# Loading the attention inputs two tokens to a row instead of four, so that VectorE's transposes write every second element

## The chip, the cores and the metric

The kernel runs on one core of a Trainium2 chip. The metric is the device time of one execution in microseconds, lower is better. Times of the kernel before are the median of three runs; the traces are single executions taken by the hardware profiler.

## The reference

A gated linear attention (a state of 48 x 48 for each head, decayed by `f` and fed with `k v`) is followed by a SwiGLU feed-forward block. There are 4 batch elements, 8 heads, 768 tokens of 48 channels; the feed-forward block has 3072 tokens, a width of 384 and a hidden width of 1536. All data are float32.

```python
f = 1.0 / (1.0 + np.exp(-f_logit))
for t in range(S):
    state = f[:, :, t, :, None] * state + np.einsum('bhd,bhe->bhde', k[:, :, t], v[:, :, t])
    y[:, :, t] = np.einsum('bhd,bhde->bhe', q[:, :, t], state)
x = y.transpose(0, 2, 1, 3).reshape(B * S, H * D)
g = x @ w_gate
out = (g * (1.0 / (1.0 + np.exp(-g))) * (x @ w_val)) @ w_out
```

## The kernel before

**Tiling.** The 768 tokens are cut into six chunks of 128, numbered 0 to 5. A unit is one chunk of one batch element; this document writes unit (2,0) for chunk 2, batch element 0. The attention of a unit works on channels by tokens: each of the tensors f, k and q lies as 128 partitions (two heads of 48 channels, padded to 64) by four head pairs by 128 tokens. Decays within a chunk are cumulative products (the scans at L577 and L601), scores are kT by qT products on TensorE (tile `sc`, L620), masked by VectorE (L633), and the result goes into `xT`, the transposed input of the feed-forward block. The state is carried from chunk to chunk (tile `decayed`, L541; update L708).

**Bringing tokens to channels.** In memory a token's 48 channels are contiguous. For chunks 0 and 1, f, k and q are loaded token by token (L433) and transposed by TensorE (L552). From chunk 2 on (`c >= SQUARES`) they are loaded into three rooms named `squares`, one for each of f, k and q and shared by all units, so that VectorE can transpose them in squares of 32 x 32 (L566 for f, L573 for k, L604 for q). A room row holds, for each head pair, a run of four successive tokens (`NI = 4`, 192 numbers); partition t of 32 holds tokens 4t to 4t+3. Four DMAs fill a room, one for each of four groups of 32 partitions (two heads, two halves of the channels), each with 32 partitions by 4 head pairs. VectorE's transpose turns the t of a square into the free dimension, so a square's 32 outputs are tokens i, 4+i, 8+i and so on: it writes every fourth element of a row (`in_turn`). The sigmoid of f is taken by ACT on the loaded room (L557), before the transpose.

**Loads.** `load_after(u)` follows the transpose of q of unit u in program order. It asks SP for f, then k, then q of unit u + 1. Each goes into the room that unit u's transpose of the same tensor has just read, and SP waits for that. All loads of this kind, the DMAs that copy a unit's result `yT` to `xT` (L669, ten for each of batch elements 0 to 2), the loads of v (L433), half of the output (L1067), and for six units the way of kT through DRAM (`turn`, L597, and back as `kt`, L629), are issued by SP in one fixed order. Each DMA also takes the next of eight completion semaphores in turn, over SP's and ACT's DMAs together, and waits until the DMA that had it before has landed.

For batch element 3 the result comes by another way: `decayed` is spread into a tile `diagonal` (cleared by POOL at L545, filled by ACT at L547), which feeds the y matmuls of L679. `diagonal` and `yT` are tiles of the same name in a pool of one buffer, so the clearing waits until the DMAs of L669 have read batch element 2's `yT`.

For turned units, kT is transposed by VectorE into qT's buffer (L594), sent to DRAM from there, and q's transpose (L604) may overwrite that buffer only after the four DMAs of L597 have landed.

**The feed-forward block.** For chunks 1 to 5, each of four groups of hidden columns is computed with fifteen smaller products (L959) on sums of tokens and of weights; ACT copies the results out of PSUM (L964), VectorE adds them up (L860, L863), ACT applies the SiLU (L975) and VectorE multiplies (L911). The down projection has seven products (L1058, L1121), whose results ACT and VectorE also add up. The sums of tokens of a chunk (`xs`, L860 to L866) are made by VectorE just before the chunk's first product.

**The order.** While TensorE computes the feed-forward block of chunk c - 1, the attention of chunk c is woven in by hand: `CHAINS`, `SCORES` and `times` give each step of a unit a place in TensorE's time line. From chunk 1's feed-forward on, `in_order` fixes the order of the instructions of PE, DVE, ACT, POOL and SP as written.

Of the kernel before, what the change touches and what calls it, by code (L numbers as in the profile page):

```python
# [289 lines left out]
def short_path(ctx, tc, ident, least, judge, q, k, v, f_logit, moe_w_gate, moe_w_val, moe_w_out, out):  # L290
# [9 lines left out]
    nc = tc.nc  # L300
    B, H, S, D = q.shape
    C = 128
    NCH = S // C
    HP = H // 2
# [90 lines left out]
    Q = 32  # L395
    NI = C // Q
    RUN = NI * D

    rooms = {}
# [6 lines left out]
    def v_of(u):  # L406
        return vs[u % (NV if units[u][1] < SQUARES else NV // 2)]

    def squares(nm):
        return rooms[nm][:, Q:Q + HP * RUN].rearrange("t (a i e) -> t a i e", a=HP, i=NI)[:, :, :, 0:Q]  # L410

    def in_turn(t):

        return t.rearrange("p a (t i) -> p a i t", i=NI)

    def load(u, what="fkqv"):
        b, c = units[u]
        rows = slice(c * C, (c + 1) * C)
        for nm, src in (("f", f_logit), ("k", k), ("q", q), ("v", v)):
            if nm not in what:  # L420
                continue
            if nm == "v":
                dst = v_of(u)
            elif c < SQUARES:
                dst = raw[nm][u % NRAW]
            else:
                for n in range(4):
                    at = Q * (1 - n % 2)
                    nc.sync.dma_start(
                        out=rooms[nm][Q * n:Q * (n + 1), at:at + HP * RUN].rearrange("t (a e) -> t a e", a=HP),  # L430
                        in_=src[b, n // 2::2, rows, :].rearrange("a (t i) d -> t a (i d)", i=NI))
                continue
            nc.sync.dma_start(out=dst[:, :, 0:D], in_=src[b, :, rows, :].rearrange("h t d -> t h d"))  # L433

# [95 lines left out]
    def attention(u):  # L530
# [25 lines left out]
        if c >= SQUARES:  # L556
            nc.scalar.activation(squares("f"), squares("f"), AF.Sigmoid)  # L557
            if b == (c > SQUARES):

                nc.scalar.activation(spare, spare, AF.Silu)  # L560
        else:
            p = transposed("fTp", fr)
            nc.scalar.activation(pairs(gate)[:, :, 1:N1], p, AF.Copy if u in ahead else AF.Sigmoid)
        yield
        if c >= SQUARES:
            nc.vector.transpose(in_turn(pairs(gate)[:, :, 1:N1]), squares("f"))  # L566
# [5 lines left out]
        if c >= SQUARES:  # L572
            nc.vector.transpose(in_turn(kT), squares("k"))  # L573
# [29 lines left out]
        if c >= SQUARES:  # L603
            nc.vector.transpose(in_turn(qT), squares("q"))  # L604
            load_after(u)
# [96 lines left out]
        if c >= SQUARES and u + 2 < len(units):  # L702
            load(u + 2, "v")
# [7 lines left out]
    def load_after(u):  # L711

        w = u + (1 if units[u][1] >= SQUARES else 2)
        if w < len(units) and (units[w][1] >= SQUARES) == (w == u + 1):
            load(w, "fkqv" if units[w][1] < SQUARES or w == SQUARES * B else "fkq")
# [449 lines left out]
    for u in range(NRAW):  # L1165
        load(u, "fkq")
# [198 lines left out]
```

## Time and profile before

| | us |
|---|---|
| median of three runs | 612.46 (612.24 to 613.02) |
| profiled execution, first to last instruction (its span) | 611.2 |
| TensorE busy in the span | 594.2 |
| VectorE busy | 499.2 |
| ACT busy | 286.7 |
| issue of one load of L429 on SP, median | 0.43 |
| landing of a load of L429 after its issue, median of f, k, q | 2.7, 2.6, 2.3 |

Of the profiled execution the trace gives the span and no time around it; the median of the timed runs is 1.26 us above the span, and this difference is used below where a span is turned into a time. Times in the trace are counted from the first instruction. Chunk 0 fills the first 147 us together with the loading of the weights; the feed-forward blocks of chunks 1 to 5 follow, about 93 us each. In a chunk the fifteen-product part comes first, then the down part. The loads that the change touches run from 137 to 471 us.

A row of the timeline gives start, duration, engine, line, operation, tiles, and in brackets how long the engine had been idle and what ended that. A row of the groups gives the count, then after the bar the summed time in us, the mean of one in ns, and the idle time before them. "x4" on SP merges four issues.

### The profile page before, as it was taken

The numbers are of one execution on the slowest core, as the hardware profiler recorded it, in microseconds if no ns is written. First come the engines' busy times: TensorE is split into PE (matmuls) and PEld (weight loads), VectorE is DVE, ScalarE is ACT, GpSimd is POOL, SyncE is SP. The second block draws the span as 40 slices with busy tenths as digits, with TensorE's granted clock in tenths as the row PEclk, the third lists the DMA queues.
The fourth block names the chain that finished last, engine by engine and source line by source line (L and its number), as shares of the span: only waits on it lengthen the run. The fifth ranks groups of instructions, "written<-read, shape, count | busy, mean of one in ns | idle before, by whom it ended". The sixth has DMA issues, their size and how long they took to land.

```text
span 611.2 us, 10816 instructions
## 1 busy us (share of the span) xinstructions
PE 594.2 (97%) x4036; PEld 487.9 (80%) x4036; DVE 499.2 (82%) x882; ACT 286.7 (47%) x530; POOL 7.6 (1%) x52
## 2 busy tenths in 40 slices
PE   7799999999999999999999999999999999999996
PEld 4654545566888799888899988899988899988896
DVE  7999989878999996999996889996879991566731
ACT  2465646313776522476732366742276730366600
POOL 1000000000000000000000000000000000000000
PEclk9999999999999999999999999999999999999999
DMA  9999582005323134424235344145313100100001
GB/s 149 249 213 284 174 250 79 1 14 154 89 52 69 27 95 113 118 54 96 53 95 122 104 111 111 31 114 118 105 51 90 27 6 10 53 1 2 0 1 58
DMA packets 109143, 54.10 MB, mean 89 GB/s; under 512 B 68761, under 2 KB 102169, under 8 KB 109081
## 3 DMA queue, kind: packets, MB, share of 16 engines
q1 hardware_dynamic: 107064, 50.56, 34.6%
q10 hardware_dynamic: 2016, 2.75, 1.2%
q8 instruction: 34, 0.56, 0.4%
q14 instruction: 29, 0.23, 0.1%
HBM read 44.04 MB, written 6.29 MB: 82 GB/s over the span
## 4 chain that ended last, share of the span: by engine, by line
PE 67%; DVE 9%; DMA 3%; issue 3%; ACT 3%; SPq 2%; ACTq 0%; POOL 0%; DVEq 0%; POOLq 0%
PE o L1058 15%; PE A L959 14%; PE B L959 11%; PE o L959 5%; PE o L780 5%; PE c L959 5%; PE o L1121 3%; PE sc L620 3%; PE y L658 2%; SPq L669 1%; DVE c L863 1%; PE y L679 1%; PE y L654 1%; PE dS L699 1%; DMA xT<-yT 1%
## 5 line engine op out<-in xcount | busy, mean ns | idle before, releaser
L1058 PE MATMUL o<-w_out,h 128*128 128x192 f32 x360 | 62.0, 327 | 0.5 <-DVE h L911 0.5
L959 PE MATMUL A<-xs,w_both 128*128 128x256 f32 x240 | 62.1, 381 | 0.0
L1058 PEld LDWEIGHTS o<-w_out,h 128*128 128x128 f32 x360 | 58.7, 190 | 1.7 <-DVE h L911 0.8
L964 ACT COPY c<-A 128x512 f32<-128x512 f32 x40 | 23.4, 584 | 61.3 <-PE A L959 61.3
L959 PEld LDWEIGHTS A<-xs,w_both 128*128 128x128 f32 x240 | 44.9, 190 | 6.5
L860 DVE TENSOR_TENSOR c<-c,aside 128x512 f32<-128x512 f32 x60 | 41.7, 694 | 9.8 <-ACT aside L964 8.4
L964 ACT COPY aside<-A 128x512 f32<-128x512 f32 x60 | 35.1, 586 | 30.9 <-PE A L959 30.9
L911 DVE TENSOR_TENSOR h<-h,c 128x256 f32<-128x256 f32 x100 | 41.3, 422 | 6.9 <-ACT h L975 6.8
L975 ACT ACTIVATE h<-c 128x256 f32<-128x256 f32 x100 | 39.4, 418 | 9.5 <-DVE c L860 5.8
L863 DVE TENSOR_TENSOR c<-c,aside 128x512 f32<-128x512 f32 x60 | 41.5, 692 | 2.0 <-ACT aside L964 1.7
L959 PE MATMUL B<-xs,w_both 128*128 128x256 f32 x160 | 41.2, 380 | 0.8 <-ACT aside L964 0.8
L1058 PE MATMUL o<-ws,h 128*128 128x192 f32 x240 | 41.5, 328 | 0.2 <-DVE A L633 0.2
L959 PE MATMUL c<-xT,w_both 128*128 128x256 f32 x160 | 41.2, 380 | 0.5 <-DVE c L863 0.5
L959 PE MATMUL A<-xs,extra 128*128 128x256 f32 x160 | 41.2, 380 | 0.0
L959 PE MATMUL B<-xT,extra 128*128 128x256 f32 x160 | 41.1, 379 | 0.0
L964 ACT COPY aside<-B 128x512 f32<-128x512 f32 x60 | 35.1, 586 | 11.4 <-PE B L959 6.9
L1058 PEld LDWEIGHTS o<-ws,h 128*128 128x128 f32 x240 | 39.1, 190 | 0.8 <-DVE A L633 0.4
L633 DVE TENSOR_TENSOR A<-sc,causal 128x512 f32<-128x512 f32 x48 | 30.8, 684 | 9.9 <-PE sc L620 9.8
L863 DVE TENSOR_TENSOR c<-o,c 128x512 f32<-128x512 f32 x40 | 27.8, 694 | 10.3 <-ACT h L975 5.8
L959 PEld LDWEIGHTS B<-xs,w_both 128*128 128x128 f32 x160 | 30.2, 190 | 5.2 <-ACT aside L964 1.2
L959 PEld LDWEIGHTS c<-xT,w_both 128*128 128x128 f32 x160 | 30.3, 190 | 5.0 <-DVE c L863 0.9
L959 PEld LDWEIGHTS A<-xs,extra 128*128 128x128 f32 x160 | 30.3, 190 | 4.4 <-ACT c L964 0.3
(140 smaller groups left out, 1138.8 us busy)
## 6 DMA issues: line engine op xcount, KB each, us to landing
fsquares<-in_f_logit_dram SPq DMA_DIRECT2D x64, 96.0 KB, 2.7
ksquares<-in_k_dram SPq DMA_DIRECT2D x64, 96.0 KB, 2.6
qsquares<-in_q_dram SPq DMA_DIRECT2D x64, 96.0 KB, 2.3
v<-in_v_dram SPq DMA_DIRECT2D x24, 192.0 KB, 3.2
w<-in_moe_w_gate_dram SPq DMA_DIRECT2D x6, 768.0 KB, 6.4
w<-in_moe_w_val_dram SPq DMA_DIRECT2D x6, 768.0 KB, 5.3
w<-in_moe_w_out_dram SPq DMA_DIRECT2D x6, 768.0 KB, 5.7
out_dram<-ob ACTq DMA_DIRECT2D x14, 192.0 KB, 2.3
```

The source lines that it names most:

```text
L620: nc.tensor.matmul(sc[par][:, a * C:(a + 1) * C], lhsT=kT[r, a, :], rhs=qT[r, a, :], start=True, stop=True)
L633: nc.vector.tensor_tensor(A[:, par], sc[par].rearrange("p (a t) -> p a t", t=C), causal.unsqueeze(1).broadcast_to((128, HP, C)), ALU.mult)
L658: nc.tensor.matmul(place(a, par), lhsT=v_[:, 2 * a + par, :], rhs=A[:, par, a, :], start=False, stop=a >= HP - 2, skip_group_check=True)
L780: nc.tensor.matmul(p, lhsT=hidden_tile(h, n // 2)[:, n % 2 * 2 + b // 2, b % 2 * C:(b % 2 + 1) * C], rhs=w_out[:, j, :], start=(n == 0), s ...
L860: nc.vector.tensor_tensor(dst, a, b, ALU.add)
L863: nc.vector.tensor_tensor(dst, a, b, ALU.subtract)
L911: lagging.append(lambda: f(*args))
L959: nc.tensor.matmul(p[name][:, n, :], lhsT=weights_of[a][:, n, j, :], rhs=tokens[b], start=fresh and n == 0, stop=True, skip_group_check=True)
L964: nc.scalar.copy(t, p[name])
L975: nc.scalar.activation(dst, src[:, 0, :], AF.Silu)
L1058: nc.tensor.matmul(p[:, n, :], lhsT=lhsTs[j][:, n * C:(n + 1) * C], rhs=rhs[:, j, :], start=first and j == order[0] and n == 0, stop=j == ...
L1121: nc.tensor.matmul(p, lhsT=hidden_tile(h, j)[:, 2, n * C:(n + 1) * C], rhs=b22[:, j, :], start=j == order[0], stop=j == order[-1])
```

## The change

A half chunk of 64 tokens is loaded at a time. Partition t of 32 then holds tokens 2t and 2t+1 of the first half and the same of the second, next to each other, so that a row in the room is as long as before. A contiguous run in memory is two tokens, 384 bytes, where it was four, 768. Each of f, k and q of a unit is loaded by eight DMAs instead of four, each with half the bytes and the same number of rows. A square's 32 outputs are tokens i, 2+i, 4+i and so on of one half: the transposes write every second element. Squares, transposes and everything after them have the same sizes and the same order. The loads for 16 units (chunks 2 to 5) are 384 DMAs where they were 192.

```diff
     def squares(nm):
-        return rooms[nm][:, Q:Q + HP * RUN].rearrange("t (a i e) -> t a i e", a=HP, i=NI)[:, :, :, 0:Q]
+        return rooms[nm][:, Q:Q + HP * RUN].rearrange("t (a j i e) -> t a j i e", a=HP, j=2, i=NI // 2)[:, :, :, :, 0:Q]
 
     def in_turn(t):
 
-        return t.rearrange("p a (t i) -> p a i t", i=NI)
+        return t.rearrange("p a (j t i) -> p a j i t", j=2, i=NI // 2)
...
                 for n in range(4):
                     at = Q * (1 - n % 2)
-                    nc.sync.dma_start(
-                        out=rooms[nm][Q * n:Q * (n + 1), at:at + HP * RUN].rearrange("t (a e) -> t a e", a=HP),
-                        in_=src[b, n // 2::2, rows, :].rearrange("a (t i) d -> t a (i d)", i=NI))
+                    to = rooms[nm][Q * n:Q * (n + 1), at:at + HP * RUN].rearrange("t (a j e) -> t a j e", a=HP, j=2)
+                    for j in range(2):
+                        some = slice(c * C + j * C // 2, c * C + (j + 1) * C // 2)
+                        nc.sync.dma_start(out=to[:, :, j, :],
+                                          in_=src[b, n // 2::2, some, :].rearrange("a (t i) d -> t a (i d)", t=Q))
```

## The prediction

> **What bounds the kernel now.** I read the page's busy shares first, then the busy time by stretches, then the chain of waits, and only then single engines.
>
> ```profile
> PE 594.2 (97%) x4036; PEld 487.9 (80%) x4036; DVE 499.2 (82%) x882; ACT 286.7 (47%) x530; POOL 7.6 (1%) x52
> ```
>
> TensorE is busy 97% of 611.2 us. All that a faster VectorE can bring is TensorE's idle time, so the question is where that lies. The answer by stretches (us; busy time of PE, weight loads, DVE, ACT, POOL; clock; DMA share; GB/s):
>
> ```profile
> 137.00:215.00 78.00, 76.14 (x457) 62.02 (x453) 73.85 (x128) 46.60 (x89) 0.56 (x6) 1.00 0.30 77
> 215.00:246.00 31.00, 30.73 (x295) 29.01 (x292) 23.94 (x41) 6.56 (x14) 0.63 (x3) 1.00 0.48 114
> 246.00:307.00 61.00, 61.00 (x394) 52.29 (x393) 57.05 (x106) 39.19 (x76) 0.21 (x2) 1.00 0.32 77
> ```
>
> The changed loads run from 137 to 471 us. From 246 us TensorE has no gap. Only in 137 to 215 does it lose 1.86 us, and there VectorE is busy 73.85 of 78. TensorE's own rows name what ended those gaps:
>
> ```profile
> 194.43 1.13 PE L959 MATMUL B<-xs,w_both 128*128 128x256 f32 x4 [0.75 <-ACT aside L964]
> 201.21 1.13 PE L959 MATMUL c<-xT,w_both 128*128 128x256 f32 x4 [0.47 <-DVE c L863]
> 210.76 1.57 PE L1058 MATMUL o<-w_out,h 128*128 128x192 f32 x8 [0.50 <-DVE h L911]
> ```
>
> The ACT copy in the first row itself waited 2.16 us for a VectorE sum, so all three are VectorE backlog. Next the chain of waits (start, us, what), around the last batch element of chunk 2:
>
> ```profile
> 228.21 0.65 ACT fsquares L557
> 228.85 0.32 SPq L669
> ...
> 234.45 0.59 SPq L669
> 235.04 0.04 issue
> 235.08 1.80 DMA xT<-yT
> ...
> 237.06 0.43 POOL diagonal L545
> ...
> 237.52 0.36 ACT diagonal L547
> ...
> 237.92 2.12 PE y L679 x56
> ```
>
> The tile `diagonal` shares one buffer with `yT`. POOL may clear it only when ten DMAs have copied `yT` away, and TensorE's y matmul waits for it. TensorE's previous row is 2.11 us from 235.73, so it ends at 237.84: nothing is to spare. What SP did before those ten:
>
> ```profile
> 222.82 1.95 SPq L429 DMA_DIRECT2D fsquares<-in_f_logit_dram  x4
> 224.87 1.80 SPq L429 DMA_DIRECT2D ksquares<-in_k_dram  x4
> 226.77 1.80 SPq L429 DMA_DIRECT2D qsquares<-in_q_dram  x4
> 228.66 7.01 SPq L669 DMA_DIRECT2D xT<-yT  x10
> ```
>
> `yT` was ready at 225.93 (ACT's copy, 0.77 from 225.16). The ten DMAs began 2.7 us later because SP was issuing the twelve loads of unit (3,0). The changed build keeps that order: f, k and q of (3,0), now 24, stand ahead of the ten.
>
> [...] Groups by shape (busy, mean ns of one):
>
> ```profile
> L604 DVE STREAM_TRANSPOSE qT<-qsquares 128x512 f32<-128x512 f32 x16 | 18.1, 1129 | 6.1 <-DMA turn<-qT 6.1
> L594 DVE STREAM_TRANSPOSE qT<-kT 128x512 f32<-128x512 f32 x6 | 4.2, 705 | 0.0
> L474 DVE SCALAR_TENSOR_TENSOR top<-w,top 128x768 int32<-128x768 int32 x6 | 5.7, 954 | 0.1
> L860 DVE TENSOR_TENSOR hs<-h 128x768 f32<-128x768 f32 x10 | 9.6, 962 | 0.0
> ```
>
> [...] writes 16 bytes apart take 1129 ns, contiguous ones 705. L474 reads every second word and is no slower than L860, which reads none so; a write of every second word is not in the trace. [...] an issue on L429 takes 0.43 us (median), its data land 2.3 to 2.7 us later. [...] a run of four tokens is 768 B, one of two 384 B. DMA share is at most 0.48 in the stretches above and the bytes stay the same, so I charge nothing for it, and up to 1 us for the range.
>
> **The change, part by part**, against the profiled execution (span 611.2; the median is 612.46, and I add the 1.26 at the end).
>
> *Transposes.* 48 (16 units, f, k, q) go from 1.12 us (mean of 1115, 1117 and 1129) to some 0.71, as L594: 48 x 0.41 = 19.7 us of VectorE. Bounds: nothing gained, or all. Where VectorE isn't the limit this is worth nothing, which from 246 us on is everywhere. In 146 to 211 the chain runs through VectorE; nine transposes lie there, 3.7 us, but TensorE can return no more than it loses: the three gaps above, 1.7, and 0.54 at 160.09 (matmul sc waits for qT). With what is lost in matmuls stretched to 1.13 I take at most 2.6 (four triples of fifteen products at 0.86 are 51.6, attention matmuls 5.5, the recurring short stall 0.14 x 4; 57.7 of 59.8 from 147.7 to 207.5, and 0.5 at 210.76).
>
> *The first k load.* Every DMA takes one of eight completion semaphores in turn, ACT's too, and waits for the DMA eight before it. In the new build k's fifth and seventh DMA of unit (2,0) get those of ACT's first and second output (L802). SP's f load at 148.50 stood on the first of them, so k's fifth goes at 148.5, its seventh near 149.6, its last near 150.4, landing (2.3) near 152.6. k's transpose started at 151.16, so VectorE is held 1.4 us; three shorter transposes give back 0.8 before sc at 160.09 (f's is lost in an ACT wait at 150.56). Sc is thus late by about 0.6, and TensorE with it. Of the 2.6 the 0.54 is then not regained, so about 1.9 is, and the stage nets 0.6 - 1.9 = -1.3. Bounds: -2.6 (k lands in time), +0.5 (it lands 2 us later).
>
> *Twelve more issues before xT at 228.66.* A half load has as many rows (32 partitions x 4) as a whole one. Issue time does not follow bytes: L669 moves 8 to 24 KB and takes 0.59, v 192 KB and 0.53. So each half costs SP what a load does: 1.95 + 1.80 + 1.80 = 5.55 more, and the ten start at 234.2. All behind shifts: last landing, POOL, ACT, y at 243.4. The third of the ten took 1.38 against 0.59, perhaps waiting behind the loads; that 0.8 may vanish. I take **+5.3**; bounds 4.5 and 5.6. Behind y on TensorE are dS, the last down products and the next chunk's first product, so the shift runs to the end.
>
> *The same place at chunks 3 and 4.* There xT was not held by loads: at 315.32 and 408.78 it started when `yT` was done. Chunk 3: f and k of (4,0) from 305.56 take 3.9 each, q then 3.6, so xT starts near 316.9. It took 7.26 for ten, of which 0.7 to 1.3 is a wait that is then over, so kt and turn come 0.4 late. Turn holds the q transpose, which ended in sc at 333.08 with nothing to spare; the shorter transpose repays 0.4. Behind it f and k of (4,1) issue until 336.7, and k's transpose is held from 335.74 to 338.9, with the token sums behind it on VectorE: 339.89 becomes about 341.9, first needed at 342.07. In all **+0.3**; bounds 0 and 2. Chunk 4: xT 1.5 late, POOL clears at 418.1 where y comes at 424.09; k's transpose 1.6 late, the sums on time. Nothing.
>
> *Elsewhere* f, k and q wait for data that were long there (q of (4,1) waits for turn), and ACT's later sigmoids lie in idle time (7.25 us of waiting at 332.80). The added semaphore waits, two more instructions a transpose at 0.05 us, pass while VectorE works off earlier operations; uncovered, 48 x 0.1 = 4.8 us of VectorE, again in its slack.
>
> *Sum:* -1.3 + 5.3 + 0.3 = +4.3. Span 615.5; time 612.46 + 4.3 = **616.8 us**.
>
> **The rivals.**
> 1. *Transposes gain, the queue does not bite* (0.10). If a half load's issue took under 0.11 us, twelve would cost less than the 1.3 gained. For it: VectorE bounds 146 to 211. Against: 0.43 for every L429 issue, whatever the tensor, and 0.5 to 0.6 for lines of fewer bytes. Time, at no cost of the queue and a gain of 1.3 to 2.6: 612.46 - 2.0 = 610.5. It decides if y at 237.92 comes no later than now.
> 2. *Every second element is as slow as every fourth* (0.10). No write in the trace excludes it. Then VectorE's 1.4 us of waiting for k stays: +1.4 + 5.3 + 0.3 = 619.5.
> 3. *SP falls behind at every chunk* (0.15): k and f of the next unit land 2 us later than I work out, and token sums are late at 342 and 435. +0.5 + 5.5 + 2.5 + 2 = 623. For it: f and k issues of 4.11 and 4.91 us at 326.62 and 418.36, and SP's rows from 342 to 435 add up to 60 of 93 us, with 48 more issues at 0.45 to 82. Against: that still fits, and worked through by SP's rows no load there lands more than 0.3 us after it is wanted.
> 4. *Gain and cost cancel* (0.04): 612.5, if k is in time and part of the ten DMAs' wait vanishes.
>
> **How the numbers follow.** The forecast has 0.61. Its own bounds give -2.6 + 4.5 = +1.9 to +0.5 + 5.6 + 2 + 1 = +9.1, the inner part of it 614 to 619. With rival 2 inside and rivals 1 and 3 mostly outside the range is 613.5 to 620.5. Under 0.2% (1.2 us) a measurement of this kernel can't be told from no change. Faster 0.10, same 0.04, slower 0.86.
>
> **What would show it.** Transposes near 0.71 us; 24 issues of about 0.43 to 0.49 ahead of xT; y of the last unit of chunk 2 some 4 us later, with TensorE idle about 5 before it and released by ACT's diagonal copy; k's first transpose waiting for its DMA; no new gap from 250 us but under 1 near 340. I am wrong if TensorE has no gap before that y, if a half load's issue is near 0.2, or if new gaps stand in 342 to 524.

## The result, and the profile after

| | before | after |
|---|---|---|
| median of five runs, us | 612.53 (612.24 to 613.02) | 628.87 (627.55 to 631.89) |
| ratio, 95% interval | | 1.0268 (1.0249 to 1.0287) |
| span of the profiled execution, us | 611.2 | 625.8 |
| VectorE busy, us | 499.2 | 482.8 |

The changed kernel is slower by 16.4 us (2.68% of 612.5), where 4.3 was predicted. VectorE's busy time has indeed fallen, by chance also by 16.4 us (the durations of the 48 transposes add up to 33.9 us where they were 53.8), and TensorE idles more. The busy shares of the changed kernel:

```profile
PE 597.4 (95%) x4036; PEld 489.2 (78%) x4036; DVE 482.8 (77%) x882; ACT 286.1 (46%) x530; POOL 7.5 (1%) x52
```

The load is now L432, and all lines behind it are two higher than before (the transposes are L568, L575, L606). Its transposes by shape (busy, mean ns of one, idle time ahead of them and what ended it):

```profile
L575 DVE STREAM_TRANSPOSE kT<-ksquares 128x512 f32<-128x512 f32 x16 | 11.3, 708 | 4.8 <-DMA qsquares<-in_q_dram 2.9 <-DMA ksquares<-in_k_dram 2.0
L606 DVE STREAM_TRANSPOSE qT<-qsquares 128x512 f32<-128x512 f32 x16 | 11.2, 700 | 12.7 <-DMA fsquares<-in_f_logit_dram 9.1 <-issue 3.6
```

Every second element is written as fast as a contiguous row (700 ns, where the contiguous writes of L596 take 703 here; every fourth element took 1129 before for the same tensor). But the idle time ahead of them has grown: q's transposes waited 6.1 us for `turn` before and now wait 12.7.

Where TensorE idles, by stretches (busy time of PE, weight loads, DVE, ACT, POOL; clock; DMA share; GB/s):

```profile
137.00:215.00 78.00, 73.92 (x406) 59.66 (x406) 68.96 (x126) 43.94 (x85) 0.40 (x5) 1.00 0.33 77
215.00:246.00 31.00, 25.15 (x238) 23.68 (x236) 20.25 (x35) 5.87 (x12) 0.57 (x3) 0.98 0.31 68
342.00:401.00 59.00, 55.88 (x382) 48.06 (x376) 46.05 (x90) 31.93 (x60) 0.32 (x3) 1.00 0.42 98
```

TensorE loses 4.1, 5.9 and 3.1 us in these. Before, it lost 1.9 in the first and next to nothing from 246 us on. In the first stretch VectorE is busy for 4.9 us less than before, and yet TensorE has lost time. What TensorE waited for (us in total, times, longest):

```profile
PE y L681 <- ACT diagonal L549: 5.7, 1, 5.7
...
PE kt L626 <- DVE state L710: 1.7, 1, 1.7
...
PE A L961 <- ACT c L966: 1.3, 1, 1.3
PE o L1060 <- ACT ob L1086: 1.2, 2, 0.7
PE o L1123 <- DVE c L862: 1.2, 1, 1.2
```

Only the first of these was predicted. SP's rows ahead of it look as the prediction drew them:

```profile
224.71 3.85 SPq L432 DMA_DIRECT2D fsquares<-in_f_logit_dram  x8
228.65 4.19 SPq L432 DMA_DIRECT2D ksquares<-in_k_dram  x8
232.94 3.70 SPq L432 DMA_DIRECT2D qsquares<-in_q_dram  x8
236.74 6.21 SPq L671 DMA_DIRECT2D xT<-yT  x10
```

24 issues of some 0.49 us each stand ahead of the ten `xT` DMAs, which start 8.1 us later than before.

The delay can be followed through the run. The table gives the start of the same TensorE rows after, minus their start before (us, from the time lines of the two profiled executions):

| row | first product of chunk 1 | sc (2,0) | sc (2,2) | y (2,3) | sc (3,0) | sc (4,0) | sc (4,1) | sc (4,2) | sc (5,0) |
|---|---|---|---|---|---|---|---|---|---|
| after | -0.63 | +0.76 | +1.83 | +7.41 | +8.55 | +9.64 | +12.26 | +13.96 | +14.75 |

These are single executions, the fastest of five for the changed kernel. The delay grows in four places: in chunk 1's products (2.5 us up to sc (2,2)), at y (2,3) (5.6), just behind it (1.1), and from the end of chunk 3's units through those of chunk 4 (6.2 between sc (3,0) and sc (5,0)).

Two of the waits come from no queue. On ACT the sigmoid of unit (2,0), with the table load behind it, stood ahead of chunk 0's output copies before:

```profile
141.56 0.63 ACT L557 ACTIVATE fsquares<-fsquares 128x512 f32<-128x512 f32 x1 [4.25 <-DMA fsquares<-in_f_logit_dram]
...
148.97 0.59 ACT L964 COPY c<-A 128x512 f32<-128x512 f32 x1 [0.89 <-PE A L959]
```

Now it stands behind them. ACT's rows after:

```profile
148.49 0.63 ACT L559 ACTIVATE fsquares<-fsquares 128x512 f32<-128x512 f32 x1 [1.05 <-DVE ob L803]
149.14 1.28 ACT L562 ACT_TABLE_LOAD   x1
...
150.54 0.57 ACT L966 COPY c<-A 128x512 f32<-128x512 f32 x1
```

The first product of chunk 1 is done before 148.5, but the copy that has to read its PSUM bank (a piece of the memory that TensorE writes its results to) before the fourth product adds to it comes at 150.54, and TensorE idles 1.33 us for it. Chunk 0's output copies are not in the hand-fixed order, which begins with this sigmoid, and the scheduler placed the two differently against each other. And `kt` of unit (2,1) was given the PSUM bank of `dS` of unit (2,0), which VectorE's state sum L710 frees late. Before, it had another of the three banks of its pool. Nothing in the diff names either, and the sentence above that everything after the transposes keeps its order doesn't hold for ACT.

### The profile page after: what moved, and what is told of

Read it like the earlier page. It is cut to its first block, busy times and chain, and to the rows that moved or that the text cites. A ratio compares the mean times of both kernels' runs of the same rounds, so it can differ in the third digit from the quotient of the medians.

```text
span 625.8 us, 11120 instructions
## 1 busy us (share of the span) xinstructions
PE 597.4 (95%) x4036; PEld 489.2 (78%) x4036; DVE 482.8 (77%) x882; ACT 286.1 (46%) x530; POOL 7.5 (1%) x52
## 2 busy tenths in 40 slices
DMA packets 136793, 54.13 MB, mean 86 GB/s; under 512 B 120984, under 2 KB 129816, under 8 KB 136728
## 4 chain that ended last, share of the span: by engine, by line
PE 64%; DVE 9%; SPq 7%; ACT 3%; issue 3%; DMA 1%; ACTq 0%; DVEq 0%; POOL 0%; POOLq 0%
PE A L961 15%; PE o L1060 12%; PE B L961 12%; PE c L961 5%; PE o L961 5%; PE o L782 5%; SPq L432 4%; PE o L1123 3%; PE sc L622 3%; SPq L671 2%; PE y L660 2%; DVE c L865 1%; PE y L681 1%; PE y L656 1%; PE dS L701 1%
## 5 line engine op out<-in xcount | busy, mean ns | idle before, releaser
L862 DVE TENSOR_TENSOR c<-c,aside 128x512 f32<-128x512 f32 x60 | 41.0, 683 | 10.0 <-ACT aside L966 8.5
L865 DVE TENSOR_TENSOR c<-c,aside 128x512 f32<-128x512 f32 x60 | 40.9, 682 | 2.1 <-ACT aside L966 1.8
L961 PEld LDWEIGHTS B<-xT,extra 128*128 128x128 f32 x160 | 30.2, 190 | 5.5 <-ACT c L966 1.3
```

The source lines that it names most:

```text
L862: nc.vector.tensor_tensor(dst, a, b, ALU.add)
L865: nc.vector.tensor_tensor(dst, a, b, ALU.subtract)
L961: nc.tensor.matmul(p[name][:, n, :], lhsT=weights_of[a][:, n, j, :], rhs=tokens[b], start=fresh and n == 0, stop=True, skip_group_check=True)
```

## The experiments

Each kernel ran beside the kernel before on the same chip; a ratio is to that, with its 95% interval. 0.001 is 0.6 us; differences in us between runs are worked out from the ratios.

### Half loads in one chunk at a time

The layout is chosen for each unit by a condition, so that part of the units are loaded and transposed as before. The diff is that of chunk 2; the others have `c == 3`, `c == 4` and `c == 2 and b > 0`:

```diff
+    def halved(u):
+        b, c = units[u]
+        return c == 2
...
+                    if not halved(u):
+                        nc.sync.dma_start(
+                            out=rooms[nm][Q * n:Q * (n + 1), at:at + HP * RUN].rearrange("t (a e) -> t a e", a=HP),
+                            in_=src[b, n // 2::2, rows, :].rearrange("a (t i) d -> t a (i d)", i=NI))
+                        continue
```

> Half loads and two-token rows for units (2,1), (2,2) and (2,3) alone; every other unit is loaded and transposed as before. ACT's order stays that of the kernel before (the sigmoid of unit (2,0) ahead of chunk 0's output copies), while the score transposes kt of unit (2,1) take the PSUM bank they take in the changed kernel. Theory (the cost of the changed kernel is a sum of local ones): nothing is lost at the start of chunk 1's products and nothing at the diagonal; the gain of shorter transposes in 146 to 211 us is largely eaten by the wait of kt of unit (2,1) for a bank (1.7 us). Time 611.5 to 613. As my prediction had this stage: about 1.9 us faster, 610.3 to 611.2. If each doubled load costs wherever it is: slower, above 613.5.

> Half loads for all four units of chunk 2, none later. The same as the run for (2,1) to (2,3), but unit (2,0) is also loaded in halves, and with that ACT's order becomes that of the changed kernel: the sigmoid of (2,0) stands behind chunk 0's output copies. Theory: the late sigmoid costs 1.5 to 2.5 us at the start of chunk 1's products, so 613.5 to 615.5, and some 2 us above the run without (2,0). Rival (my prediction's reason: only the ring of completion semaphores delays k): at most 0.5 us above the run without (2,0).

> Half loads for the four units of chunk 3 alone. Twelve more issues stand ahead of xT of unit (2,2), and nine groups of twelve more in chunk 2's products. Theory: 5.6 us of waiting for the diagonal, 1.1 us of slower y matmuls after that idle time, 0.3 elsewhere: +7, 619.5, bounds 618.5 to 620.5. Rival (the y matmuls were slow by chance): 618. Rival (SP's backlog from chunk 2's own half loads is part of the wait): below 617.

> Half loads for the four units of chunk 4 alone. Theory: SP falls behind where chunk 3 is handed to chunk 4 and through chunk 3's products: 0.8 before the first scores of chunk 4, 2.6 before its second y, 1.7 by the end of the products: +5, 617.5, bounds 615.5 to 618.5; q's transposes of (4,0), (4,1) and (4,2) wait for turn and f's for loads. My prediction had 0.3, so 612.8. Rival (the loss there is carried over from backlog of chunks 2 and 3): below 614.

| half loads in | ratio | us |
|---|---|---|
| (2,1), (2,2), (2,3) | 1.0020 (1.0011 to 1.0029) | +1.2 |
| chunk 2 | 1.0046 (1.0033 to 1.0060) | +2.8 |
| chunk 3 | 1.0136 (1.0120 to 1.0153) | +8.3 |
| chunk 4 | 1.0087 (1.0072 to 1.0102) | +5.3 |

Chunks 2, 3 and 4 add up to 16.4 us, all of the 16.4 of the change, to within some 2 us by the intervals. The losses are local: chunk 4 alone costs its 5.3 without any backlog from chunks 2 and 3. That refutes the rivals of the last two runs. Chunk 5's loads had no run of their own. They are not quite free: in the changed kernel TensorE falls back by 0.8 us between sc (4,2) and sc (5,0), 0.53 of it in one wait, where the run with chunk 4 alone loses nothing. In the profile of the chunk 3 run the gap before y (2,3) is 6.04 us and sc (3,0) comes 7.04 late; its measured +8.3 is a little above the theory's bounds.

The chunk 2 runs went worse than the theory: three units with faster transposes and nothing behind them to delay, and still slower than before. TensorE's rows in the run with (2,1) to (2,3):

```profile
182.21 0.88 PE L638 MATMUL kt<-idf,kT 128*128 128x128 f32 x4 [1.73 <-DVE state L722]
182.88 1.92 PE L973 MATMUL A<-xs,w_both 128*128 128x256 f32 x4
184.59 1.66 PE L973 MATMUL B<-xs,w_both 128*128 128x256 f32 x4
```

The wait of `kt` for its bank is there, and the two products behind it take 1.92 and 1.66 us where they take 1.03. These slow products are no part of the median: the profiled execution was the slowest of 13, 2.8 us above their median, and in the run with all of chunk 2 the same wait is followed by products of 1.03 us. That each doubled load costs something wherever it is would also give +1.2; the next section tells the two apart. Adding unit (2,0) costs 1.6 us more (1.0046 against 1.0020, with some 1.0 of uncertainty), as the theory of the late sigmoid had it: in that run ACT has the order of the changed kernel, and the interval between the first product of chunk 1 and sc (2,0) is 1.4 us longer than before.

### The bank and ACT's order, put back

The bank of each tile of the three-bank pool can be set by hand: three tags of one buffer each, and a list of what the other build had chosen.

```diff
+    BANKS = "576576576576756765765675675675675675675675675675675"
+    taken = []
     def bank(name):
...
+        taken.append(name)
+        return banks[-1].tile([128, 512], FP32, tag="b" + BANKS[len(taken) - 1], name=name)
```

For ACT, the order of the sigmoid, the table load, chunk 0's output copies and DMAs and the first copy of chunk 1's products is fixed as it was:

```diff
                 nc.scalar.activation(spare, spare, AF.Silu)
+                if u == SQUARES * B:
+                    keep_order([traced[-1], *out_steps])
```

> The run with half loads for (2,1) to (2,3), with one thing undone: each tile of the pool of three PSUM banks gets, by name, the bank it has in the kernel before, so that kt of unit (2,1) no longer takes the bank of dS of (2,0). Theory (the bank is what eats the gain): kt waits for nothing, its 1.73 us go, and the slow products after it (1.92 and 1.66 us for 1.03) go too; what is left is the gain of the shorter transposes, 0.8 to 1.9 us under the kernel before: ratio 0.997 to 0.9987. Rival (the shorter transposes gain nothing even so, since VectorE's backlog comes from other work): ratio 0.9995 to 1.0005. Rival (the three units' own 36 more issues cost): ratio stays at 1.002.

> The kernel before with nothing changed but the bank of each tile of that pool: those of the changed kernel. Theory: kt of unit (2,1) waits some 1.9 us for VectorE's state sum of (2,0); VectorE catches up meanwhile, so that TensorE's later gaps of 0.75, 0.47 and 0.50 shrink, and the end is 0.5 to 1.9 later: ratio 1.001 to 1.003. Rival (the wait only takes the place of the later gaps): ratio 1.000.

> The changed kernel with all its half loads, with the two side effects of scheduling undone: the sigmoid of (2,0) stands ahead of chunk 0's output copies on ACT again, and the banks are those of the kernel before. Theory: the start of chunk 1's products loses nothing (1.4 us less), kt of (2,1) waits for nothing (1.8 us less), and all else stays: some 3 us under the changed kernel, ratio to the kernel before 1.020 to 1.0235, and the first L1060 down product of chunk 1 starts 0.5 to 2 us earlier than in the kernel before. Rival (k of (2,0) is late whatever ACT does): 1.5 to 2 us under it, and the score matmul of (2,0) still waits 0.6 or more.

| | ratio |
|---|---|
| (2,1) to (2,3) halved, old banks | 0.9989 (0.9980 to 0.9998) |
| kernel before, new banks | 1.0034 (1.0021 to 1.0047) |
| changed kernel, old banks and old ACT order | 1.0199 (1.0172 to 1.0226) |

The banks alone, with no load and no transpose changed, cost the kernel before 2.1 us, more than expected. TensorE's rows of that run:

```profile
180.96 0.63 PE L630 MATMUL kt<-idf,kT 128*128 128x128 f32 x4 [1.73 <-DVE state L714]
...
196.25 1.13 PE L965 MATMUL B<-xs,w_both 128*128 128x256 f32 x4 [0.72 <-ACT aside L970]
...
203.02 1.13 PE L965 MATMUL c<-xT,w_both 128*128 128x256 f32 x4 [0.45 <-DVE c L869]
...
212.57 1.57 PE L1064 MATMUL o<-w_out,h 128*128 128x192 f32 x8 [0.51 <-DVE h L917]
```

The last three are the gaps of 0.75, 0.47 and 0.50 us that the prediction called VectorE backlog. VectorE has been given 1.7 us to catch up here, and they are still 0.72, 0.45 and 0.51. They are not a backlog that is carried along, then, but short chains between neighbouring steps (a sum, a copy, a product) that follow TensorE wherever it is.

With the old banks the three faster units gain 0.7 us instead of losing 1.2. So 36 more issues alone cost nothing here; that the transposes gain is only just clear of the noise in this run. The changed kernel with both effects undone stands 0.7% (4.2 us by the ratios, with 2.0 of uncertainty; 3.2 by its sc (5,0), which starts 12.24 late from a first product 0.09 late) below the changed kernel. There sc (2,2) is 0.8 us earlier than before. The rival of a late k of (2,0) falls: its scores come 0.2 us nearer to the first product than before.

### The number of DMAs against the size of their runs

```diff
-                    nc.sync.dma_start(
-                        out=rooms[nm][Q * n:Q * (n + 1), at:at + HP * RUN].rearrange("t (a e) -> t a e", a=HP),
-                        in_=src[b, n // 2::2, rows, :].rearrange("a (t i) d -> t a (i d)", i=NI))
+                    to = rooms[nm][Q * n:Q * (n + 1), at:at + HP * RUN].rearrange("t (a e) -> t a e", a=HP)
+                    for j in range(2):
+                        nc.sync.dma_start(
+                            out=to[:, 2 * j:2 * j + 2, :],
+                            in_=src[b, n // 2 + 4 * j:n // 2 + 4 * j + 3:2, rows, :].rearrange("a (t i) d -> t a (i d)", i=NI))
```

> The kernel before with each of the 192 loads split in two by head pairs: the layout, the runs of four tokens (768 bytes), the transposes of every fourth element, ACT's order and the PSUM banks stay those of the kernel before; only the number of DMAs doubles, as in the change. Theory (the number of issues, not the size of a run, is what costs): the diagonal, chunk 3 and chunk 4 cost what they cost in the changed kernel, and nothing is repaid by shorter transposes: ratio 1.019 to 1.026. Rival (runs of 384 bytes, twice as many packets, are to blame): 1.005 to 1.012.

Measured: 1.0241 (1.0225 to 1.0256), nearly the 1.0268 of the whole change, with runs of 768 bytes and the slow transposes. The gap before y (2,3) is 5.71 us, sc (5,0) 13.00 late. The number of issues is what costs, not the shorter runs: the DMA packets are 112217 here, 109143 before and 136793 in the changed kernel. This build also kept ACT's order and the banks of the kernel before: what moved those was the new layout, not the doubling. Against the changed kernel with those two undone (1.0199), which differs from it in the layout, the new layout, with its shorter transposes, is worth 2.6 us over the whole run, with some 1.9 of uncertainty.

### SP's order at the diagonal

```diff
-            load_after(u)
+            if (b, c) == (B - 1, 2):
+                load(u + 1, "f")
+            else:
+                load_after(u)
...
                     f += n
+            if (b, c) == (B - 2, 2):
+                load(u + 2, "kq")
```

This is the second of the three; the third has "fk" and "q" in these places, and the first put off the call of unit (2,2) as a whole.

> The changed kernel with one move on SP: the 24 loads of unit (3,0) are issued behind the ten xT DMAs of unit (2,2), not ahead of them. Theory: POOL clears the diagonal some 7 us earlier, the y matmuls of (2,3) wait for nothing and take 2.1 us, not 3.27: 5.6 + 1.15 = 6.7 us less than the changed kernel, ratio to the kernel before 1.014 to 1.017, unless the later loads of (3,0) hold VectorE: they land 2 to 6 us later than now, and the scores of (3,0) have room for about that. Rival (the y matmuls' 3.27 us have nothing to do with the idle time): 5.6 less and y at 3.2.

> The changed kernel with SP's order altered around unit (3,0) only: its 8 loads of f stay ahead of the ten xT DMAs of unit (2,2), its 16 of k and q come behind them. Theory: xT starts at about 228.7 where it started at 236.74, POOL clears the diagonal in time, y of (2,3) waits for nothing and takes 2.1 us, not 3.27; k of (3,0) lands about 6 us later than now and may cost up to 2 us of that again on VectorE: ratio to the kernel before 1.015 to 1.0195 (the changed kernel: 1.027). Rival (y's 3.27 us have nothing to do with the idle time): y without a gap and at 3.2. Rival (the diagonal waits for something else than SP's queue): y's gap of 5.7 stays and the ratio is 1.026 to 1.028.

> The changed kernel with only the 8 loads of q of unit (3,0) moved behind the ten xT DMAs of unit (2,2); its 16 of f and k stay ahead. Theory (the stretch has more issues than time, but an order can be found in which both waits are short): xT starts near 232.9 where it started at 236.74, the gap before y of (2,3) shrinks from 5.7 to about 1.9, k of (3,0) lands as in the changed kernel, q is in time: 3.7 us less, and up to 1.1 more if y's matmuls are quick again; ratio to the kernel before 1.0185 to 1.021, below the 1.0233 of the run that moved k too. Rival (every order costs the same, since SP has no time for 24 more issues there): 1.0225 to 1.027.

The first of these moved the wrong loads: those of (3,0) are asked for by the step of unit (2,3), and this kernel put off (2,3)'s own, behind the transposes that read them. The kernel then ran its second, general path as well, which it has for decays that are too small: 1749 us, from which nothing follows.

With k and q behind `xT`: 1.0233 (1.0219 to 1.0248), 2.1 us under the changed kernel where 4.5 to 7 were expected. The gap before y is gone and y takes 1.75 us, but VectorE's rows show where it went:

```profile
242.38 0.71 DVE L575 STREAM_TRANSPOSE kT<-ksquares 128x512 f32<-128x512 f32 x1 [9.23 <-DMA qsquares<-in_q_dram]
```

The DMA named is the one that came last by the profile; this transpose reads k, whose loads are issued from 236.46 here. VectorE's order is fixed, and the sums of the down products stand behind k's transpose. A down product on TensorE then waits for a sum that has to read its bank first:

```profile
250.03 3.67 PE L1128 MATMUL o<-w_out,h 128*128 128x192 f32 x12 [2.50 <-DVE c L867]
```

With q alone behind it: 1.0214 (1.0192 to 1.0236), 3.3 us under the changed kernel, at the upper edge of what was expected; k comes as there, and y waits 1.60 us, close to the expected 1.9. The two runs can't be told apart by their times (intervals of some 1 us and more each). So an order helps, but each serves one consumer at the cost of another: at 0.49 us an issue, 24 loads and ten `xT` DMAs take some 18 us of SP here.

### The way of kT through DRAM

```diff
-        turned = (SQUARES + 1) * B + 1 < u < (NCH - 1) * B
+        turned = False
```

> Half loads for the four units of chunk 4 alone, and no unit takes the way of kT through DRAM: kt of the six turned units is made by TensorE's transposes and an ACT copy instead, as for the other units. To be read against the kernel before with the same taken away. Theory (the loads of chunk 4 are late because they stand behind turn's DMAs in the ring of completion semaphores, and because kt and turn, which SP issues late, land late): the half loads cost at most 1.5 us here, where they cost 5.3 with turn; ratio of the two 1.000 to 1.0025. Rival (SP is late by the issues alone): 4 to 6 us, ratio 1.0065 to 1.0095.

> The kernel before without the way through DRAM: six more units transpose kT on TensorE (four transposes of some 0.12 us each) and copy it on ACT. Control for the run before it in this list. Both theories: 24 transposes add about 3 us to a TensorE that has no gap there: ratio 1.003 to 1.008.

With half loads in chunk 4: 1.0025 (1.0014 to 1.0035). Without: 1.0038 (1.0024 to 1.0052). The half loads, which cost 0.87% with `turn`, cost nothing without it; the difference of -0.13% is within the intervals. The transposes of chunk 4 wait for twice as many DMAs there too, so these added waits on VectorE cost nothing that shows. What VectorE waited for between 320 and 400 us in the chunk 4 run with `turn`:

```profile
DVE qT L618 <- DMA fsquares<-in_f_logit_dram: 9.4, 2, 5.2
DVE gates L580 <- ACT fsquares L571: 2.8, 1, 2.8
DVE qT L618 <- issue: 1.9, 1, 1.9
...
DVE kT L587 <- DMA ksquares<-in_k_dram: 1.2, 1, 1.2
```

The DMA named in the first row came last by the profile, but q's transpose doesn't read f: it needs the four `turn` DMAs, which landed at about the same time. Without `turn` no transpose waits more than 0.2 us there, and TensorE has no wait from 300 to 435 us. In the time line of the run with `turn`, SP's rows around the first of the waits are:

```profile
325.80 0.61 SPq L643 DMA_DIRECT2D kt<-turn  x1
326.51 2.63 SPq L611 DMA_DIRECT2D turn<-qT  x4
329.19 6.20 SPq L444 DMA_DIRECT2D fsquares<-in_f_logit_dram  x8
```

The eight issues of f take 6.20 us where eight without `turn` ahead take 3.84, so f of (4,1) arrives late at ACT's sigmoid (the 2.8 us), and its transpose holds the sums behind it. But the wait behind `turn` is not new at this place. Before:

```profile
323.26 0.60 SPq L629 DMA_DIRECT2D kt<-turn  x1
323.96 2.61 SPq L597 DMA_DIRECT2D turn<-qT  x4
326.62 4.11 SPq L429 DMA_DIRECT2D fsquares<-in_f_logit_dram  x4
```

Four issues of f took 4.11 us there, some 2.2 more than four usually take (1.95), and now it is some 2.4 more. New are the four more issues, and that SP comes to `turn` 2.6 us later. `kt` stood 0.70 us ahead of `turn` before as well, and `turn` landed 5.6 us after its issue (median of four; 4.5 in the run with chunk 4). At the `turn` of unit (4,2) it is otherwise. There 4.7 us lay between `kt` and `turn` before, `turn` landed after 2.2, and f behind it took 2.06 us for four. In this run `kt` is issued 0.69 us ahead, `turn` lands after 5.5, and f behind it takes 6.12 for eight.

So two things were measured: SP comes late to `kt`, `turn` and f by its own issues, and where that brings `kt` right ahead of `turn`, the data of `turn` come later and the issues of f behind them take longer. The ring of completion semaphores, which the expectation named, is not what holds the first of these issues: in the changed kernel it takes 1.82 us at 337.44 and 2.30 at 386.69 (0.43 is the median), and the `xT` DMAs that had the same semaphores before had landed at 333.60 and 383.23. What does was not shown. What each of the two is worth was not taken apart: without `turn`, SP also has 30 DMAs less to issue.

A third path shows in the changed kernel's rows where chunk 3 is handed to chunk 4:

```profile
335.07 0.71 ACT L549 COPY diagonal<-decayed 48x192 f32<-48x192 f32 x2 [10.51 <-POOL diagonal L547]
335.80 0.48 ACT L1086 COPY ob<-o 128x384 f32<-128x384 f32 x1
336.34 4.17 PE L1060 MATMUL o<-ws,hs 128*128 128x192 f32 x24 [0.71 <-ACT ob L1086]
```

Late `xT` DMAs hold POOL, POOL holds ACT's copy into the diagonal, and an output copy stands behind that on ACT, whose bank a down product waits for. Before, that copy ended at 325.54, 1.1 us ahead of the product. In the run with chunk 4 the wait is 1.31 us, and without `turn` it is gone.

### A version that beats both

Half loads where VectorE's time counts and no queue is short: chunk 2, with ACT's order and the banks put back and q's loads of (3,0) behind `xT`. Chunks 3 to 5 stay as before.

> Half loads for the four units of chunk 2 alone, the sigmoid of (2,0) ahead of chunk 0's output copies, the banks of the kernel before, and q's loads of unit (3,0) behind the xT DMAs of (2,2). Theory: nothing is lost; the shorter transposes are worth 0.5 to 1.2 us: ratio 0.998 to 0.9992. As my prediction had it, 1.9 or more: below 0.997. Rival (k of (2,0), loaded in halves, is late and eats it): 0.9995 to 1.001.

> The same without unit (2,0): half loads for (2,1), (2,2) and (2,3) alone, the banks of the kernel before, and q's loads of (3,0) behind the xT DMAs of (2,2). Theory: 0.2 us less than the run without that move, in which y of (2,3) waited 0.20 us for the diagonal: ratio 0.998 to 0.9992. Rival (q of (3,0) comes late behind xT): 0.9995 or more.

Measured: 0.9975 (0.9967 to 0.9983), 611.57 us beside 613.09 for the kernel before, and 0.9985 (0.9978 to 0.9992) without unit (2,0). The first is a little better than expected. The busy shares of the first, and its gaps left of the three:

```profile
PE 595.7 (98%) x4036; PEld 489.9 (80%) x4036; DVE 495.6 (81%) x882; ACT 286.2 (47%) x530; POOL 7.6 (1%) x52
```

```profile
194.45 1.13 PE L990 MATMUL B<-xs,w_both 128*128 128x256 f32 x4 [0.41 <-ACT aside L995]
...
210.43 1.57 PE L1091 MATMUL o<-w_out,h 128*128 128x192 f32 x8 [0.55 <-DVE h L942]
```

0.75 has become 0.41, 0.47 no longer shows, 0.50 has stayed. sc (2,2) comes 0.9 us earlier, counted from the first product. That is what the faster transposes bring: under half of the 1.9 taken. Not all of the gain is theirs. In both runs another 0.5 us is won between sc (2,2) and sc (3,0), where q's loads were moved; with the old banks and no such move (2,1) to (2,3) lost 0.1 there. The move alone, in the kernel before, was not run.

## Why the prediction was wrong

The sign was right, and the mechanism of the largest term too. The sum was too small by 12 us. Its three terms against the runs with one chunk in halves:

| place | predicted | measured |
|---|---|---|
| start of chunk 1's products to 211 us (chunk 2's loads) | -1.3 | +2.8 |
| `xT` ahead of y (2,3) (chunk 3's loads) | +5.3 | +8.3 |
| the same place at chunks 3 and 4 (chunk 4's loads) | +0.3 | +5.3 |

By its own steps:

- **Transposes, 1.12 to 0.71:** right (0.70 to 0.71). **Worth 1.9 of at most 2.6:** wrong; 0.8 to 0.9 in chunk 1. The step took TensorE's three gaps for VectorE backlog that any VectorE time saved would buy back. The run with new banks in the old kernel shows that they are not. The 0.54 at 160.09 was idle time of the weight loads; with that wait gone, sc (2,0) came only 0.2 us nearer to the first product.
- **The first k load, 0.6, and the stage's net -1.3:** this is the step that failed first. The ring of semaphores was looked at, and the order of the instructions on ACT and the banks of the pool were taken for unchanged. The stage cost +2.8. The late sigmoid is worth 1.6 of it and the bank some 1.9 (from 1.0020 to 0.9989). The ring did hold k's loads as the step had it: their eight issues took 9.15 us and ended at 149.66, and the fifth, after 5.21 us without an issue on SP, went at 147.82, when ACT's output DMA that had its semaphore before had landed at 147.80. (In this trace the DMAs of SP and ACT share eight such semaphores; of the 485 for which the landing of the DMA before on the same one is known, none was issued ahead of it.) But what k's transpose followed was a sum that waited for ACT. That sc (2,0) came 0.76 late, near the 0.6 of the step, is luck. With both effects undone, k of (2,0) delays nothing.
- **Twelve more issues before xT, +5.3:** right as a wait: 5.57 in the changed kernel, 5.96 in the chunk 3 run. Missed behind it: TensorE ran slower after the gap, y at 3.27 us instead of 2.12 (+1.15; 1.5 up to sc (3,0) in the chunk 3 run). The other 0.8 of the +8.3 is in no row of that run's profile, which is the fastest of its four executions.
- **Chunk 3's end, +0.3, chunk 4 and elsewhere nothing:** the second failed step. Measured +6.2 from sc (3,0) to sc (5,0), and +5.3 in chunk 4's run. The 24 issues of (4,0) took 12.9 us in that run where the step put 11.4, so `kt` and `turn` came over 2 us late and not 0.4. It held POOL's clearing against y alone, when ACT's output copy stands behind the diagonal and a down product waits for it (0.71 and 0.53 us in the changed kernel). It held k's transpose against the token sums alone ("first needed at 342.07"), when the sum c of L862 stands behind the same transpose, and a down product (L1123) waits for that sum's bank (1.23 us). The wait of f behind `turn` it had: its 336.7 holds the 4.11 us. But it assumed that `turn` lands as soon as before, and that of (4,2) landed after 5.1 us instead of 2.2.
- **Rivals:** the third, SP falling behind at every chunk, came nearest with 623. It had the places from 342 on, but no term for the scheduler and none for the clock. The first and second fell with the first profile, the fourth (gain and cost cancel) with the time.

What the prediction named as proof against itself, new gaps in 342 to 524, is what the profile shows.

## What to carry to other kernels

A change to loads also changes what a scheduler decides: compare the order of every engine and the banks and buffers of every pool before costing anything, since here a bank alone cost 2.1 us. Price an issue queue by its count of DMAs at each consumer, with what stands in the same queue behind slow DMAs, not by its mean load over a stage (doubling the count alone gave a ratio of 1.0241 of the 1.0268). Look at everything that stands behind a late instruction in its engine's order, not only at the one step that is known to need it. And idle time of TensorE that an engine ended is worth that engine's saving only if the wait is a backlog; give the engine a little time elsewhere and see if the gap closes (here 1.7 us on VectorE left 0.75, 0.47 and 0.50 at 0.72, 0.45 and 0.51).

## What the runs showed of the hardware that was not expected

After an idle time of TensorE its matmuls can run at half speed. From 140 us on, in the profiled executions here, gaps of 5.7 to 6.3 us were followed by slow matmuls four times of four (the first y rows 1.66 us instead of 1.12), gaps of 1.6 to 2.5 us four times of ten (1.92 and 1.66 for 1.03; 3.67 for 2.11), gaps of 1.3 to 1.4 us never in six. Each time it cost 1.1 to 2.4 us more. In the changed kernel the granted clock is 0.50 from 244.73 us, in the last part of the gap of 5.66 us ahead of y (2,3), to 248.15, that is for 3.41 us. In the run with (2,1) to (2,3) the mean clock is 0.79 from 180 to 188 us, and in the chunk 3 run 0.77 and 0.80 in the two stretches of 8 us from 236; at a clock of 0.50 that is some 3.4 and 6.9 us of lowered time. Gaps of 1.73 us were followed by slow matmuls three times of six, so a gap that short is no safe one. What decides whether a short gap brings the drop was not found; it makes single executions differ, so a cost read from one profile has to be held against the median.

Runs of 384 bytes in place of 768 did not slow the loads: their data landed 2.0 us after the issue, against 1.9 for DMAs of the same size with runs of 768 bytes (the run that only splits the loads) and 2.3 to 2.7 for the whole loads before. So the shorter runs show no cost at the DMA shares of 0.31 to 0.42 in the stretches above. An issue took 0.43 us (median) for half the bytes as for the whole.
